# Gated linear attention into a multiplicative FFN on one core: K transposed by DMA instead of TensorE, state scaling on ScalarE, one block's products regrouped

## The chip, the cores and the metric

The kernel runs on one core of a Trainium2 chip. The metric is the device time of one execution in microseconds. Five engines work side by side, each through its own instructions in the order in which they were written: TensorE (PE; its weight loads are shown apart as PEld), VectorE (DVE), ScalarE (ACT), GpSimd (POOL), and SyncE (SP), which here issues every DMA. An instruction that waits holds up all that stands behind it on its engine.

## The reference

The first half is an attention with a gated state, the second a feed-forward block on its output. Sizes: batch 4, 8 heads, 768 tokens, head dimension 48; d_model 384, d_ff 1024; all in float32.

```python
f = 1.0 / (1.0 + np.exp(-f_logit))
for t in range(S):
    state = f[:, :, t, :, None] * state + np.einsum('bhd,bhe->bhde', k[:, :, t], v[:, :, t])
    y[:, :, t] = np.einsum('bhd,bhde->bhe', q[:, :, t], state)
x = y.transpose(0, 2, 1, 3).reshape(B * S, H * D)     # 3072 tokens by 384
a = x @ w1
b = x @ w2
h = a * b @ w3
out = h @ w_out
```

## The kernel before

**Attention.** The 3072 tokens are cut into 24 chunks of 128 (6 chunks make one batch element). A chunk's q, k and gate logits lie as 112 partitions (two heads of 48, the second from partition 64 on) by 512 columns (4 head pairs by 128 tokens). VectorE makes the running products of the gates forward and backward by two scans, and from them the scaled tiles Q and K (lines 545 and 559). The recurrence then becomes matmuls: K against Q gives the scores within a chunk (`pairs`), the masked scores A against v give the values inside the chunk (`values`), the state of the chunk before against Q gives the rest (`from_state`), and K against v gives the state's growth (`update`). The last of these sums over tokens, so it needs K with the tokens on partitions: a tile `kt`, 128 tokens by 4 x 112 columns. In the kernel before, TensorE turns K round with four transposes against an identity into a PSUM bank (`turn`, line 598), and ScalarE copies that bank to `kt` (line 731).

From chunk 4 on the matmuls of one chunk stand together with the next chunk's in one uninterrupted stretch on TensorE, called a visit here (`visit` in `rest`): values of chunk u, scores of chunk u+1, values again, the state's part, and the update of chunk u+1. So the visit of chunk u waits for Q, K and `kt` of chunk u+1. After it ScalarE copies the result (`outcome`, line 849) and the next scores (`taken`, line 707), GpSimd masks those (line 713), VectorE adds the state's growth (lines 763 and 766), and VectorE multiplies the state by the chunk's gate product G, one number per row and head pair (`state`, line 822). The result of a chunk goes through DRAM to be laid out anew as x for the FFN (lines 870 and 873).

**FFN.** The tokens form 6 blocks of 512. w3 and w_out are folded into one matrix early (line 1471). The up products (x by w1 and w2) of a block are then done in one of three ways: block 0 plainly (line 902), later ones by schemes with fewer products. `seven` (line 998) takes two column tiles of the hidden layer and makes their products with 22 matmuls of 128 by 256; a block has four such groups. `many` (line 1153) takes four column tiles with 40 such matmuls; a block has two such groups. `many` needs sums of weight columns (line 1114), which are kept in tiles that the attention used before, so it can start only once the attention is nearly through; the list `homes` names these tiles. In the kernel before, blocks 1 and 2 use `seven`, blocks 3 to 5 use `many`, and block 2 (counted from 0; `MANY - 1`, the third block) is mixed: two groups of `seven` and one of `many`. The down products (`down`, line 902 with 128 by 192) of every block use seven products for two token tiles.

**Order.** A planner in the kernel (`Plan`) lists every task with an engine, an assumed cost, what it waits for, a priority and the buffers that it takes; it then places the tasks one after the other and emits them in that order. So a changed cost or task moves others on every engine. Up to a planned time of 130 us, gaps on TensorE are filled with matmuls on a constant tile (`idle`, line 402).

**Places that the change touches:** `turning` and `turn` (K's transpose), `front` (K's buffers and the task of line 559), `state` and `outcome` in `rest`, `moves` (a DMA as a task on SP and one on the DMA engines), the `mixed` case of `ffn`, and the pools of `homes`.

Of the kernel before, what the change touches and what calls it, by code (L numbers as in the profile page):

```python
# [79 lines left out]
SURE_W = 2.0  # L80
NEED = (0.0, 1.0, 2.0, 3.0)
# [214 lines left out]
def ranged(ctx, tc, q, k, f_logit, v, w1, w2, w3, w_out, out, ident, w12, wc, left):  # L296
# [63 lines left out]
    homes += [lambda p=p, nm=nm: p.tile([P, NQ], F32, name=nm) for p, nm, n in ((one, "fwd", 1), (one, "bwd", 1), (work, "K", 2), (work3, "Q", 3), (work3, "ys", 3)) for _ in range(n)]  # L360
# [16 lines left out]
    plan.pools["t"][0:4] = [aside] * 4  # L377
# [89 lines left out]
    def moves(n, size, rate, emit, deps, prio, late=0.0, since=0.0, lanes=("lane",)):  # L467


        for j in range(n):  # L470
            i = plan.add("SP", 0.45, (lambda: None) if j else emit, [d] if j else deps, prio - j * 1e-3, takes=lanes, lag=0.85, since=since)
# [8 lines left out]
    def front(u):  # L480
# [76 lines left out]
        def scale_k():  # L557
            s["K"] = work.tile([P, NQ], F32, name="K")[0:R]
            nc.vector.tensor_tensor(s["K"], ku, s["R"], ALU.mult)  # L559

        t["k"] = plan.add("DVE", 0.72, scale_k, [t["r"], t["lk"]] + past(u, 2, "a", "t"), n0, shared=True)
# [162 lines left out]

    def turning(u):

        s, t = st[u], tk[u]

# [24 lines left out]
    def middle(u):  # L753
# [4 lines left out]
        def emit():  # L758
# [10 lines left out]
            "DVE", 0.36 if closes else 0.72, emit, [t["s"], t["m"]] + ([] if opens else past(u, 1, "d")) + past(u, 2, "v"), need(u) - 5,  # L769
        )  # L770

    def rest(u):
# [37 lines left out]
        if not closes:  # L810
# [8 lines left out]
            def state():  # L819
                gain = s["G"].unsqueeze(2).to_broadcast([R, HP, D])  # L820
                if u >= NPE:
                    nc.vector.tensor_tensor(s["S"], s["S"], gain, ALU.mult)
                    return
# [8 lines left out]
                "DVE", 0.36 if opens or u >= NPE else 0.72, state,  # L832
                [t["s"], t["G"]] + (past(u, 2, "b") if u < NPE else [t["mid"]]), n0, shared=True,
# [9 lines left out]
        def outcome():  # L843
            s["ys"] = work3.tile([P, NQ], F32, name="ys")[0:R].rearrange("p (h c) -> p h c", c=C)
            py = s["yb"] if u < NPE else s["py"][0:R, :, 0 : 2 * C]
            ys = s["ys"]
            if u >= NPE:
                ys, py = ys.rearrange("p (b r) c -> p r b c", r=2), py.rearrange("p r (b c) -> p r b c", c=C)
            nc.scalar.activation(ys, py, AF.Copy, accum_out=ysum[:, u : u + 1])  # L849
# [3 lines left out]
            "ACT", 0.8, outcome, [t["v"]] + past(u, 3, "z"),  # L853
# [35 lines left out]
        else:  # L889
            t["z"] = moves(2, 197, 300, written, [t["y"]], n0 - 100)  # L890
# [16 lines left out]
    def ffn(n):  # L907
# [655 lines left out]
    def judge():  # L1563
        low = work.tile([R, 1], F32, name="low")
        nc.vector.tensor_reduce(out=low, in_=lasts, axis=AX.XY, op=ALU.min)
        zero = work.tile([R, NU], F32, name="zero")
        nc.vector.tensor_scalar(zero, ysum, 0.0, None, ALU.mult)
        nil = work.tile([R, 1], F32, name="nil")
        nc.vector.tensor_reduce(out=nil, in_=zero, axis=AX.X, op=ALU.add)
        nc.vector.tensor_scalar(nil, nil, 0.0, None, ALU.is_equal)  # L1570
        good = work.tile([P, 1], F32, name="good")
# [11 lines left out]
    def heard():  # L1583
        row = work.tile([1, P], F32, name="row")
# [3 lines left out]
    def decided():  # L1588
        least = work.tile([1, 1], F32, name="least")
# [4 lines left out]
    for u in range(NU):  # L1594
# [13 lines left out]
        if u == NU - 1:  # L1608
            late = plan.add("none", 0.0, lambda: None)
            plan.pools["f"] += [late] * 4  # L1610
            for nm in ("y", "mid", "m", "v"):
                tk[u][nm]["frees"].append(late)
            fronts["deps"] += [tk[u][nm] for nm in ("r", "k", "q")] + [tk[u - 1]["G"]]
# [405 lines left out]
```

## Time and profile before

| | |
|---|---|
| median of 3 runs | 458.17 us (457.83 to 459.44) |
| the profiled execution's own time | 458.04 us |
| its span, first to last instruction | 456.2 us |
| PE busy | 448.7 us, 98% of the span |
| DVE / ACT / POOL busy | 371.1 / 212.0 / 69.1 us |
| granted TensorE clock | 1.00 in every stretch |
| visits that need a `kt` of chunk 7 or later | from 116.2 us to 246.9 us |
| last visit (chunk 23) starts | 251.5 us |

The profiled execution's time is its span and 1.84 us around it. Three stages are to be told apart: up to about 116 us the weights come in, are converted and folded, and the first chunks run; from there to 251.5 us the other chunks run with FFN work of blocks 0 to 2 between their visits; after that only FFN work is left, with checks on the weights' range in ScalarE's gaps. A busy share says little by itself: the question is always which engine the others wait for in a stage.

### The profile page before, as it was taken

To read this page: it belongs to the slowest core of one execution; us is meant where nothing else is said; L and a number is where in the kernel's file an instruction comes from. 1 tells how busy PE (TensorE), PEld (TensorE's weight loads), DVE (VectorE), ACT (ScalarE), POOL (GpSimd) and SP (SyncE) were. 2 spreads that over 40 slices of the span, in tenths; PEclk is the share of its full clock that TensorE was granted. 3 is DMA by queue.
4 is the path that set the end of the run, shared out by engine and by line. 5 is a ranking of instruction groups with operands and counts; after the bars stand their busy time and mean duration, and the time that the engine had idled before them with its cause. 6 is when DMAs were issued, how large, how long until landed. Compare 5 with 4: busy or idle time off the path is not lost.

```text
span 456.2 us, 11781 instructions
## 1 busy us (share of the span) xinstructions
PE 448.7 (98%) x4792; PEld 392.5 (86%) x4792; DVE 371.1 (81%) x651; ACT 212.0 (46%) x473; POOL 69.1 (15%) x90
## 2 busy tenths in 40 slices
PE   7999999999999999999999999999999999999996
PEld 6788886666899888889999888899899988889996
DVE  8997899999898999989999699885659466767641
ACT  4565344432234453443323256665665666675300
POOL 9341000131222531223223000000000000000000
PEclk9999999999999999999999999999999999999999
DMA  6897898833236666356323502446365612233111
GB/s 178 268 339 249 300 340 284 271 108 105 71 100 196 180 175 162 105 155 184 97 73 82 147 16 78 138 141 205 132 194 172 204 60 96 91 93 92 37 69 39
DMA packets 43308, 68.74 MB, mean 151 GB/s; under 512 B 5217, under 2 KB 28386, under 8 KB 42226
## 3 DMA queue, kind: packets, MB, share of 16 engines
q1 hardware_dynamic: 43250, 67.95, 48.6%
q8 instruction: 38, 0.62, 0.6%
q14 instruction: 20, 0.16, 0.1%
HBM read 58.88 MB, written 9.04 MB: 149 GB/s over the span
## 4 chain that ended last, share of the span: by engine, by line
PE 95%; DVE 1%; SPq 1%; DMA 1%; POOL 0%; issue 0%; POOLq 0%; DVEq 0%
PE f L902 25%; PE l L1153 15%; PE f L998 13%; PE f L1153 12%; PE f L1471 9%; PE l L902 9%; PE py L658 3%; PE pa L584 2%; PE f L598 2%; PE py L677 2%; PE pa L690 2%; PE f L402 1%; SPq L495 1%; DMA ab<-in_k_dram 1%; DVE K L559 0%
## 5 line engine op out<-in xcount | busy, mean ns | idle before, releaser
L713 POOL TENSOR_SCALAR_AFFINE_SELECT A<-A 64x512 f32<-64x512 f32 (+1 forms) x46 | 46.2, 1004 | 107.8 <-ACT A L707 105.7
L1471 PE MATMUL f<-place 128*128 128x384 f32 x128 | 42.4, 487 | 0.0
L902 PE MATMUL f<-xt,w 128*128 128x256 f32 x192 | 42.1, 380 | 0.0
L902 PEld LDWEIGHTS f<-xt,w 128*128 128x128 f32 x192 | 36.3, 190 | 5.0
L1471 PEld LDWEIGHTS f<-place 128*128 128x128 f32 x128 | 23.9, 190 | 15.5
L902 PE MATMUL f<-place 128*128 128x192 f32 x176 | 31.9, 327 | 0.0
L998 PE MATMUL f<-xt,w 128*128 128x256 f32 x120 | 31.3, 380 | 0.0
L551 DVE TENSOR_TENSOR_SCAN bwd<-gate,back 112x512 f32<-112x512 f32 x24 | 30.4, 1267 | 0.7
L529 DVE TENSOR_TENSOR_SCAN fwd<-gate,floor 112x512 f32<-112x512 f32 x24 | 30.0, 1251 | 1.2 <-ACT gate L521 0.3
L902 PEld LDWEIGHTS f<-place 128*128 128x128 f32 x176 | 28.9, 190 | 0.4 <-issue 0.2
L849 ACT ACTIVATE ys<-py 112x512 f32<-112x512 f32 x22 | 13.1, 597 | 32.4 <-PE py L677 29.9
L1407 ACT ACTIVATE place<-place 128x512 f32<-128x512 uint32 (+2 forms) x24 | 21.4, 890 | 9.7 <-DMA place<-in_w_dram 8.7
L998 PEld LDWEIGHTS f<-xt,w 128*128 128x128 f32 x120 | 22.5, 190 | 2.9
L902 PE MATMUL f<-wc,ab 128*128 128x192 f32 x128 | 23.6, 328 | 0.0
L813 POOL TENSOR_TENSOR G<-lasts,gate 112x4 f32<-112x4 f32 x20 | 12.3, 614 | 72.3 <-ACT lasts L534 28.7
L902 PEld LDWEIGHTS f<-wc,ab 128*128 128x128 f32 x128 | 21.2, 190 | 0.3
L521 ACT ACTIVATE gate<-f 112x512 f32<-112x512 f32 x22 | 13.9, 631 | 16.4 <-DVE bwd L551 7.2
L902 PE MATMUL l<-place 128*128 128x192 f32 x112 | 19.8, 326 | 0.0
L658 PEld LDWEIGHTS py<-A,vt 64*64 64x64 f32 (+1 forms) x672 | 13.3, 127 | 7.3 <-issue 6.3
L998 PE MATMUL f<-place 128*128 128x256 f32 x72 | 19.1, 386 | 0.0
L902 PEld LDWEIGHTS l<-place 128*128 128x128 f32 x112 | 18.5, 190 | 0.1
L658 PE MATMUL py<-A,vt 64*64 64x64 f32 (+1 forms) x672 | 18.0, 223 | 0.2
(288 smaller groups left out, 1063.4 us busy)
## 6 DMA issues: line engine op xcount, KB each, us to landing
place<-in_w_dram SPq DMA_DIRECT2D x21, 512.0 KB, 5.9
A<-in_w_dram SPq DMA_DIRECT2D x19, 512.0 KB, 4.0
place<-in_w_dram SPq DMA_DIRECT2D x8, 1024.0 KB, 6.3
q<-in_q_dram SPq DMA_DIRECT2D x46, 96.0 KB, 2.9
vt<-in_v_dram SPq DMA_DIRECT2D x23, 192.0 KB, 2.9
out_dram<-o SPq DMA_DIRECT2D x23, 192.0 KB, 2.8
k<-in_k_dram SPq DMA_DIRECT2D x44, 96.0 KB, 2.4
yt<-ys SPq DMA_DIRECT2D x44, 96.0 KB, 2.9
```

Source lines behind the costliest of these rows:

```text
L521: nc.scalar.activation(gate[u % 2][:, 0:NQ], fu, AF.Sigmoid)
L529: nc.vector.tensor_tensor_scan(s["P"], gate[u % 2][:, 0:NQ], floor, 0.0, ALU.mult, ALU.max)
L551: nc.vector.tensor_tensor_scan(s["R"][:, ::-1], gate[u % 2][:, NQ:0:-1], back[:, ::-1], 0.0, ALU.mult, ALU.max)
L658: done = nc.tensor.matmul(y_block(u, hp, par, half)[p0 : p0 + w], lhsT=s["v"][half * W : half * W + W, h * D : h * D + w], rhs=s["A"][half ...
L713: nc.gpsimd.affine_select(out=a, in_=a, pattern=pattern, compare_op=ALU.is_ge, fill=0.0, base=0, channel_multiplier=-1,)
L813: nc.gpsimd.tensor_tensor(s["G"], lasts[:, u], heads(gate[(u + 1) % 2][:, 0:NQ])[:, :, 0], ALU.mult)
L849: nc.scalar.activation(ys, py, AF.Copy, accum_out=ysum[:, u : u + 1])
L902: nc.tensor.matmul(out_, lhsT=lhs[i], rhs=rhs[i], start=start and i == 0, stop=i == len(lhs) - 1, skip_group_check=True,)
L998: nc.tensor.matmul(q[nm][:, which * TH : which * TH + TH], lhsT=lhs[i](which), rhs=rhs[i], start=start and which == 0 and i == 0, stop=i = ...
L1153: nc.tensor.matmul(banks[g, c][:, which * TH : which * TH + TH], lhsT=lhs, rhs=x_node(a), start=first and which == 0, stop=True, skip_grou ...
L1407: nc.scalar.activation(part_.bitcast(F32), part_, AF.Copy, bias=2.0, scale=2.0**-51)
L1471: nc.tensor.matmul(w3s["p", jc], lhsT=w3s[jc][:, kc * P : kc * P + P], rhs=wos[:, kc], start=(kc == 0), stop=(kc == KF - 1),)
```

## The change

From chunk 7 on (17 chunks, 7 to 23) `turning` calls a new function, `crossing`. ScalarE splits K's float32 words into 16-bit halves, first all of one half, then all of the other (`split`, into a part of tile A that is no longer used otherwise); one DMA transpose on SP's queue turns the 112 by 1024 halves into 128 by 8 x 112 (`crossed`); ScalarE puts the halves together again as `kt` (`merged`). There is one tile for the split halves and one for the transposed ones, so a split waits for the transpose before it, and a transpose for the merge before it. K gets three buffers instead of two, the results `ys` two instead of three.

The scaling of the state by G goes, from chunk 2 on, from one VectorE instruction to four ScalarE activations, one for each head pair with its own scale column (18 chunks). The third block's up products are now all by `seven`: four groups, none of `many`. The rest is what goes with it: tiles moved to make room, `homes` in a new order that the temporaries of `many` take only when the last chunks are done, and a planned margin (0.8) on the transfer of the results to DRAM.

```diff
-    diag = [t[:, 0 : 2 * HP * W].rearrange("p (r h c) -> p r h c", r=2, h=HP) for t in flat]
-    mids = [t[0:R, 2 * HP * W : 2 * HP * W + HP * D].rearrange("p (h d) -> p h d", d=D) for t in flat]
+    apart = both[0:R, 2 * (NQ + HP * D) : 2 * (NQ + HP * D) + NQ].bitcast(U16)
+    halves = keep.tile([P, HP * R], F32, name="halves").bitcast(U16)
+    diag = [both[:, i * NQ : i * NQ + NQ].rearrange("p (r h c) -> p r h c", r=2, h=HP) for i in range(2)]
+    mids = [both[0:R, 2 * NQ + i * HP * D : 2 * NQ + (i + 1) * HP * D].rearrange("p (h d) -> p h d", d=D) for i in range(2)]
...
-    plan.pools["t"][0:4] = [aside] * 4
+    held = plan.add("none", 0.0, lambda: None)
+    plan.pools["t"] = [aside] * 4 + [held] * (len(homes) - NWT)
...
-            s["K"] = work.tile([P, NQ], F32, name="K")[0:R]
+            s["K"] = work3.tile([P, NQ], F32, name="K")[0:R]
...
-        t["k"] = plan.add("DVE", 0.72, scale_k, [t["r"], t["lk"]] + past(u, 2, "a", "t"), n0, shared=True)
+        t["k"] = plan.add("DVE", 0.72, scale_k, [t["r"], t["lk"]] + past(u, 3, "a", "t"), n0, shared=True)
...
+    def crossing(u):
+        s, t = st[u], tk[u]
+        def split():
+            nc.scalar.copy(apart.rearrange("p (two n) -> p two n", two=2), s["K"].bitcast(U16).rearrange("p (n two) -> p two n", two=2))
+        def crossed():
+            nc.sync.dma_start_transpose(halves.rearrange("p (g r) -> p g r", r=R), apart)
+        def merged():
+            s["kt"] = work.tile([P, HP, R], F32, name="kt")
+            to = s["kt"].rearrange("p h r -> p (h r)").bitcast(U16).rearrange("p (n two) -> p two n", two=2)
+            nc.scalar.copy(to, halves.rearrange("p (two n) -> p two n", two=2))
+        n0 = need(u)
+        t["t"] = plan.add("ACT", 1.05, split, [t["k"]] + past(u, 1, "c2"), n0 - 50)
+        t["c2"] = moves(1, 74, 200, crossed, [t["t"]] + past(u, 1, "e"), n0 - 100, SURE_K, issue=1.23)
+        t["e"] = plan.add("ACT", 1.21, merged, [t["c2"]] + past(u, 2, "s"), n0 - 50)
...
+        if u > 6:
+            crossing(u)
+            return
...
-                    nc.vector.tensor_tensor(s["S"], s["S"], gain, ALU.mult)
+                    for hp in range(HP):
+                        nc.scalar.activation(s["S"][:, hp], s["S"][:, hp], AF.Copy, scale=s["G"][:, hp : hp + 1])
...
-                "DVE", 0.36 if opens or u >= NPE else 0.72, state,
+                *(("DVE", 0.36 if opens else 0.72) if u < NPE else ("ACT", 0.95)), state,
...
-            s["ys"] = work3.tile([P, NQ], F32, name="ys")[0:R].rearrange("p (h c) -> p h c", c=C)
+            s["ys"] = work.tile([P, NQ], F32, name="ys")[0:R].rearrange("p (h c) -> p h c", c=C)
...
-            t["z"] = moves(2, 197, 300, written, [t["y"]], n0 - 100)
+            t["z"] = moves(2, 197, 300, written, [t["y"]], n0 - 100, SURE_Z)
...
-            for jc in range(KH // 2 if mixed else KH):
+            for jc in range(KH):
                 seven(jc)
             if mixed:
-                many(1)
```

What this does to the order is shown at three places. In the rows, names with a number are single buffers of a tile; the line numbers of the changed kernel are some 5 to 31 higher than those before.

First TensorE, the end of one visit in the middle of the attention stage and what comes behind it. py is the PSUM tile of the results, pa that of the scores and the state's growth, f a bank of the FFN. Before:

```order
L658 MATMUL py<-A,vt 48x64 x2
L677 MATMUL py<-Q,S 48x64 x8
L677 MATMUL py<-Q,A 48x64 x8
L690 MATMUL pa<-vt,kt 48x48 x16
L598 MATMUL f_1930<-ident,K 128x112 x4
L998 MATMUL f_1712<-xt,place 128x256 x4
L998 MATMUL f_1811<-place,w_59 128x256
```

And the end of a visit now:

```order
L663 MATMUL py<-A,vt 48x64 x2
L682 MATMUL py<-Q,S 48x64 x8
L682 MATMUL py<-Q,A 48x64 x8
L695 MATMUL pa<-vt,kt 48x48 x16
L1027 MATMUL f_2146<-place 128x256
L1027 MATMUL f_2146<-xt,w_59 128x256
```

The four transposes (line 598 before) are gone, and FFN products follow the visit at once.

Next ScalarE, the rows of about one and a half chunks while down products of a block run as well. ys is the result, the A that is written from pa the scores, and the A that is written from K the split halves. Before:

```order
L849 ACTIVATE ys,ysum<-py 112x2x2x128
L707 COPY A<-pa 128x512
L1276 COPY place<-f_2779 128x192
L521 ACTIVATE gate_95<-f_102 112x512
L1289 COPY o<-f_2779 128x192
L534 COPY lasts<-fwd 112x4
L731 COPY kt<-f_2830 128x448
L1039 COPY place<-f_2568 128x512
L521 ACTIVATE gate_96<-f_103 112x512
```

And now:

```order
L743 COPY kt<-halves 128x2x448
L1068 COPY a_106<-f_2501 128x512
L735 COPY A<-K 112x1024
L539 COPY lasts<-fwd 112x4
L1304 COPY place<-f_2524 128x192
L851 ACTIVATE S<-S,G 112x48 x4
L1317 COPY o<-f_2524 128x192
L526 ACTIVATE gate_96<-f_103 112x512
L743 COPY kt<-halves 128x2x448
L878 ACTIVATE ys,ysum<-py 112x2x2x128
L735 COPY A<-K 112x1024
L712 COPY A<-pa 128x512
```

A merge (`kt<-halves`), a split (`A<-K`) and the four state scalings stand in ScalarE's row for each chunk; the transposed tile of one chunk is merged just ahead of the split for the next, and here both stand ahead of the copy of the scores.

Last SP's queue, the same stage in the changed kernel; the DMA to yt writes a chunk's result to DRAM, the one to xt reads it back:

```order
L738 DMA_TRANSPOSE halves<-A 128x8x112
L483 DMA vt<-in_v_dram 128x384
L500 DMA f_103<-in_f_logit_dram 48x512 x2
L899 DMA yt<-ys 48x4x128 x2
L500 DMA k_100<-in_k_dram 48x512 x2
L500 DMA q_97<-in_q_dram 48x512 x2
L500 DMA f_102<-in_f_logit_dram 48x512 x2
L902 DMA xt<-yt 128x3x128
```

One transpose for each chunk now stands among the loads and the result's two transfers; the rest of the queue has the same transfers as before, in a slightly other order.

More of the change, by code (lines that the diff above doesn't have):

```diff
@@ L80 @@
 SURE_W = 2.0
+SURE_K = 1.0
+SURE_Z = 0.8
 NEED = (0.0, 1.0, 2.0, 3.0)
@@ L1583, in heard @@
     def heard():
-        row = work.tile([1, P], F32, name="row")
+        row = one.tile([1, P], F32, name="row")
         nc.sync.dma_start(row, where["all"].rearrange("r one -> one r"))
@@ L1588, in decided @@
     def decided():
-        least = work.tile([1, 1], F32, name="least")
+        least = one.tile([1, 1], F32, name="least")
         nc.vector.tensor_reduce(out=least, in_=where["row"], axis=AX.X, op=ALU.min)
```

23 lines of the change are left out of this document (13 added, 10 removed).

## The prediction

> **What bounds the kernel now.** I read the page's busy times, slices and chain first. The chain is the work that ended last, followed back from the end.
>
> ```profile
> span 456.2 us, 11781 instructions
> ...
> PE 448.7 (98%) x4792; PEld 392.5 (86%) x4792; DVE 371.1 (81%) x651; ACT 212.0 (46%) x473; POOL 69.1 (15%) x90
> ...
> PEclk9999999999999999999999999999999999999999
> ...
> PE 95%; DVE 1%; SPq 1%; DMA 1%; POOL 0%; issue 0%; POOLq 0%; DVEq 0%
> ```
>
> TensorE is 95% of the chain at full granted clock. Then the two stages that the change touches, as busy time in a stretch (columns: length, then PE, PEld, DVE, ACT, POOL busy), and all that TensorE waited for:
>
> ```profile
> 116.20:251.50 135.30, 135.30 (x2637) 122.50 (x2636) 125.68 (x222) 53.17 (x130) 39.64 (x47) 1.00 0.49 134
> 251.50:456.20 204.70, 200.39 (x1097) 184.79 (x1096) 139.51 (x291) 108.19 (x247) 0.00 (x0) 1.00 0.35 111
> ...
> PE f L402 <- DVE floor L425: 1.7, 1, 1.7
> PE py L598 <- DVE K L559: 0.5, 1, 0.5
> PE f L598 <- DVE K L559: 0.5, 1, 0.5
> ```
>
> The first stage holds the visits from chunk 6 on; TensorE is busy in all 135.30 us of it, and all its waits in the whole kernel come to 2.7 us, none in this stage. In the second it is idle 4.3 us, at the very end, when the last outputs are stored. VectorE is close behind in the first stage (125.68 of 135.30 us), ScalarE far (53.17). So the kernel is TensorE's instruction list, and time goes only where that list gets shorter, or where it starts to wait.
>
> **The change, part by part.** *Removed: 17 groups of four transposes.* The pieces of the chain in order of time (start, length, what):
>
> ```profile
> 154.54 0.35 PE pa L690 x16
> 154.89 1.92 PE f L998 x8
> 156.81 0.38 PE f L598 x4
> 157.20 2.61 PE f L998 x12
> ...
> 161.33 0.36 PE pa L690 x32
> 161.69 0.53 PE f L598 x4
> 162.22 4.33 PE f L998 x20
> ...
> 219.67 1.74 PE f L998 x8
> ```
>
> A group costs 0.38 us amid FFN work and 0.53 us right behind a visit (whose last piece is pa L690). But eight FFN records take 1.92 us behind a visit and 1.74 us elsewhere: 0.18 us is the price of leaving a visit, and the FFN work will pay it once the transposes are gone. So a group behind a visit saves 0.35 us. In the timeline 10 of the 17 stand amid FFN work and 7 behind a visit: 10 x 0.38 + 7 x 0.35 = 6.25 us. Bounds: 17 x 0.35 = 5.95 us if all are of the cheaper kind, 17 x 0.53 = 9.0 us if the handover vanishes too.
>
> *Changed: the third block.* Two groups of `seven` (44 matmuls) replace one of `many` (40). Twenty records take 4.33 us, and a matmul has two records: 0.433 us each, so 4 x 0.433 = +1.73 us.
>
> *One saving that is given back.* Ahead of block 0's down products the planner fills a gap with matmuls on a constant, in the old order and in the new, so something other than TensorE sets the time there:
>
> ```profile
> 117.91 5.38 PE f L902 x24
> 123.29 0.86 PE f L402 x4
> ```
>
> The first of the 17 groups stands before this point, so its 0.35 us only lengthens that gap.
>
> The sum goes against the profiled execution's own 458.04 us (span 456.2 and 1.84 around it; the runs' median is 458.17): 458.04 - 6.25 + 1.73 + 0.35 = 453.9 us.
>
> *Added on ScalarE.* The trace has no copy of 16-bit halves; the nearest rows (busy us, mean ns of one):
>
> ```profile
> L731 ACT COPY kt<-f 128x448 f32<-128x448 f32 x22 | 11.8, 537 | 7.0 <-PE f L598 6.8
> L704 ACT COPY A<-pa 128x1024 f32<-128x1024 f32 x2 | 2.0, 1008 | 0.0
> L1407 ACT ACTIVATE place<-place 128x1024 f32<-128x1024 uint32 x8 | 9.3, 1165 | 7.3 <-DMA place<-in_w_dram 7.3
> L534 ACT COPY lasts<-fwd 112x4 f32<-112x4 f32 x24 | 4.8, 202 | 8.1 <-DVE fwd L529 8.1
> L1289 ACT COPY o<-f 128x192 f32<-128x192 f32 x8 | 2.5, 319 | 13.6 <-PE f L902 13.6
> L1039 ACT COPY a<-f 128x512 f32<-128x512 f32 x9 | 5.3, 585 | 5.1 <-PE f L998 4.9
> L1042 ACT COPY ab<-f 128x256 f32<-128x256 f32 x6 | 2.2, 372 | 7.5 <-PE f L998 7.5
> L713 POOL TENSOR_SCALAR_AFFINE_SELECT A<-A 64x512 f32<-64x512 f32 (+1 forms) x46 | 46.2, 1004 | 107.8 <-ACT A L707 105.7
> L822 DVE TENSOR_TENSOR S<-S,G 112x192 f32<-112x192 f32 x18 | 7.3, 404 | 0.6
> ```
>
> The split has 1024 elements a row: 1.01 us plain, 1.17 us with strided words; I take the middle, 1.09, since it reads with a stride and writes dense. The merge has 896: 0.95 us at the same rate. A state scaling of 48 columns lies between 0.20 us (4 columns) and 0.32 us (192): 0.23, four of them 0.92. The old copy of `kt` (0.54) goes. Per chunk +2.42 us, 17 times 41 us. The new order also draws 36 more matmuls of `seven` between these visits (22 go with three copies of 0.585 and one of 0.372): +3.5 us. The stage itself becomes 135.3 - 5.9 + 36 x 0.433 = 145 us. So ScalarE has 98 us of work in 145: busier than before, not full. This costs nothing as long as TensorE's other work in the list covers a copy that comes later; without that cover each chunk could lose a few tenths (a rival below).
>
> *Taken from VectorE:* 18 x 0.40 = 7.3 us. TensorE never waited for it there, so that gains nothing by itself. The scaled state comes 0.92 - 0.40 = 0.5 us later; the visit that reads it also waits for the mask, whose two GpSimd instructions take 2 x 1.0 us over the same time, and these hide it.
>
> *Added on SP and the DMA queue.* 17 transposes of 112 x 2048 bytes, 224 KB. The trace has none; its DMAs, from issue to landing:
>
> ```profile
> vt<-in_v_dram SPq DMA_DIRECT2D x23, 192.0 KB, 2.9
> xt<-yt SPq DMA_DIRECT2D x22, 192.0 KB, 3.4
> ...
> place<-in_w_dram SPq DMA_DIRECT2D x21, 512.0 KB, 5.9
> place<-in_w_dram SPq DMA_DIRECT2D x8, 1024.0 KB, 6.3
> ...
> place<-in_v_dram SPq DMA_DIRECT2D x1, 192.0 KB, 8.9
> ...
> good<-good SPq DMA_DIRECT2D x1, 0.5 KB, 7.9
> ```
>
> Below, 2.9 us (192 KB in long rows); above, 7.9 us (128 pieces of 4 bytes, the smallest pieces in the trace). Nearest is xt<-yt, short pieces and almost the size: 3.4 x 224 / 192 = 4.0 us.
>
> What it must fit into is a ring: split (one tile for the halves), transpose, merge (one tile for the result), next split. I put it at 1.09 + 4.0 + 0.95 and 0.5 us of hops = 6.5 us per chunk. The visits must be at least that far apart. A visit takes 2.08 us (0.38 + 0.47 + 0.23 + 0.45 + 0.36, and the 0.18 behind it):
>
> ```profile
> 159.80 0.38 PE py L658 x11
> 160.18 0.47 PE pa L584 x30
> 160.65 0.23 PE py L658 x16
> 160.88 0.45 PE py L677 x32
> ...
> 298.48 0.86 PE l L1153 x4
> 299.34 1.30 PE l L902 x8
> ```
>
> Between the start of chunk 9's visit and that of chunk 22's, the new order has 13 visits, 140 matmuls of `seven`, 2 of `many` (four records 0.86, so 0.43 us each) and 56 down matmuls (eight records 1.30, so 0.325 us each): 27.0 + 60.6 + 0.9 + 18.2 = 106.7 us, 8.2 us per chunk; the shortest distance is 2.08 + 10 x 0.433 = 6.4 us. A ring of 6.5 us fits, with 0.1 us short once or twice, which the second `kt` buffer evens out. So I cost the transposes at nothing; TensorE's FFN work hides them, by a margin of 1.7 us per chunk.
>
> [...]
>
> **Rivals.** *1. The ring becomes the bound (slower).* If a transpose takes longer to land, visits wait for `kt`, and with them all that stands behind in TensorE's list. For it: one tile each for halves and result, SP's one queue in which a transpose can stand behind a result's store that waits, and the 512 KB loads at 5.9 us. Against: 8.2 us between visits. At 5.9 us the ring is 8.4: the six distances from chunk 9 on average 7.7 us (78 `seven` matmuls, six visits), the last five 7.9 us, so 6 x 0.7 + 5 x 0.5 = 6.7 us are lost: 460.6 us. That is the point from which it is slower; at 6.3 us it loses 11 us: 465. I price it at 463 us.
>
> *2. ScalarE's row holds TensorE up a little (no change).* A merge and a split, 2.04 us, stand ahead of the copies of scores and FFN banks, and a late transpose holds up everything behind its merge. A `seven` group has 4 matmuls (1.73 us) between the one that ScalarE copies and the one that needs the copy (0.585): 2.04 + 0.585 - 1.73 = 0.9 us short where the pair falls right there. At once in three chunks, 17 x 0.3 = 5 us: 458.9 us. For it: 68% busy in written order. Against: the order interleaves two groups.
>
> [...] With 7.9 us, the price of the 4-byte pieces, the ring is 10.4 us: 13 x (10.4 - 8.2) = 29 us, 483 us. Against: that DMA moves 0.5 KB; all others land within 6.3 us in the median but for one load of 8.9 us in the crowded first 20 us. [...]
>
> That the change doesn't do what it says is out: in the new order the 17 groups are gone.
>
> **Numbers.** The forecast, 453.9 us, gets 0.60, with its own range from 450.7 (9.0 us saved, nothing given back) to 455.8 us. Rival 2 gets 0.18, rival 1 0.17, rival 3 0.05. What a measurement here can tell from no change is about 0.5%, 2.3 us. So faster 0.60, same 0.18, slower 0.22. The range is 450.5 to 461: it takes in rival 2 and the near half of rival 1.
>
> **What would show it.** Right: no L598 after chunk 6; TensorE without idle time between 116 us and the last visit, which starts some 9 us later than 251.5; a transpose landing near 4 us; splits and merges near 1 us; ScalarE near 98 us in the stage. Wrong: waits of py L663 or pa L695 for ACT kt L743, or visits spaced evenly at the ring's length (rival 1); waits of f L1027 for ACT copies (rival 2); landings of 8 us and more (rival 3). If the span between two visits shrinks by more than 0.38 us for a group, my price of a transpose is wrong.

## The result, and the profile after

The changed kernel takes 456.76 us (median of 11 runs, 455.17 to 458.17); the kernel before, timed in turn with it, 459.25 us (457.83 to 459.55). The ratio is 0.995, with a 95% interval of 0.9933 to 0.9966. So the change gains some 2.5 us; the interval leaves 1.6 to 3.1 us. The prediction said 453.9 us, 0.9% less than before. On two further occasions the changed kernel gave 0.9933 (0.9912 to 0.9955) and 0.996 (0.9937 to 0.9984) of before.

The first view is the page: span, busy times, DMA totals, the main DMA queue (packets, MB, share of 16 engines' span) and the chain that ended last. Of the changed kernel:

```profile
span 456.0 us, 11696 instructions
PE 445.6 (98%) x4732; PEld 388.5 (85%) x4732; DVE 357.5 (78%) x615; ACT 249.1 (55%) x557; POOL 67.2 (15%) x90
DMA packets 59086, 72.65 MB, mean 159 GB/s; under 512 B 20994, under 2 KB 44163, under 8 KB 58003
q1 hardware_dynamic: 59026, 71.85, 56.6%
PE 88%; DVE 4%; POOL 3%; DMA 1%; ACT 1%; issue 1%; SPq 1%; DVEq 0%; POOLq 0%
```

And the two DMA lines of the kernel before:

```profile
DMA packets 43308, 68.74 MB, mean 151 GB/s; under 512 B 5217, under 2 KB 28386, under 8 KB 42226
q1 hardware_dynamic: 43250, 67.95, 48.6%
```

TensorE was 95% of the chain and is now 88%; VectorE, GpSimd, ScalarE and DMA have 9% together. TensorE still stands out, but the end now also hangs on other engines. The 17 transposes bring 15,778 packets, nearly all under 512 bytes.

Next, both stages (length, then PE, PEld, DVE, ACT, POOL busy, granted clock, DMA share, GB/s) and waits inside the first one (engine, tile and line, what it waited for: us, times, longest):

```profile
118.30:265.70 147.40, 145.95 (x2646) 130.51 (x2645) 129.21 (x224) 92.09 (x206) 36.49 (x47) 1.00 0.67 146
265.70:456.00 190.30, 185.79 (x1029) 172.09 (x1028) 123.13 (x257) 100.34 (x236) 0.00 (x0) 1.00 0.37 121
...
ACT kt L743 <- DMA halves<-A: 16.4, 9, 3.4
DVE place L1001 <- DMA xt<-yt: 2.4, 1, 2.4
PE pa L589 <- DVE S L794: 0.8, 1, 0.8
PE pa L695 <- ACT kt L743: 0.5, 1, 0.5
```

The attention stage was forecast at 145 us and takes 147.4. TensorE, which waited for nothing there before, now waits for VectorE's state sum (L794) and once for `kt`; the first places to look are the two long waits above, ScalarE's for transposes (halves) and VectorE's for one gather (xt).

All stages side by side, each row from one profiled execution, with the visits' starts read from the timeline (us; chunk 3's matmuls come alone, before the joint visits):

| kernel | chunk 3 starts | to chunk 6 | to the last visit | to the end | from chunk 3 on |
|---|---|---|---|---|---|
| before | 34.1 | 82.1 | 135.3 | 204.7 | 422.1 |
| changed | 35.2 | 83.1 | 147.4 | 190.3 | 420.8 |
| changed, second occasion | 34.3 | 83.1 | 146.4 | 189.9 | 419.4 |
| changed, third occasion | 34.8 | 83.6 | 147.0 | 190.2 | 420.8 |
| transposes cut to an eighth | 34.4 | 83.4 | 144.9 | 190.0 | 418.2 |
| changed, sums later | 34.5 | 83.5 | 146.0 | 190.0 | 419.4 |
| changed, rows exchanged on SP | 34.5 | 83.6 | 146.7 | 190.0 | 420.3 |
| changed, both of these | 33.9 | 84.1 | 145.1 | 190.1 | 419.4 |
| both, again | 34.4 | 83.2 | 145.4 | 190.3 | 419.0 |

The start of chunk 3 varies by a microsecond between executions of one kernel, so the last column compares best. The forecast, 4.17 us less, would be 417.9 there. The tail fell by 14.4 to 14.8 us, since FFN work went from it into the attention stage: 68 records, or 34 matmuls, fewer in the last row of the view above than in the prediction's. The stretch to chunk 6 is one to two microseconds longer in all of them. One of these is no loss but moved work: behind chunk 3 TensorE now makes 156 records of the first block's products in one go instead of 150, and has the six fewer to make in the attention stage. Before, and in the changed kernel:

```profile
35.47 32.64 PE L902 MATMUL f<-xt,w 128*128 128x256 f32 x150
...
36.59 33.94 PE L931 MATMUL f<-xt,w 128*128 128x256 f32 x156
```

What is missing in the changed kernel lies for the most part in the third column: 1.4 to 2.4 us above the forecast 145. In its first profile TensorE counts as idle for 1.45 us of the 2.4 (147.40 less 145.95). The experiments look for the missing time.

### The profile page after: what moved, and what is told of

Its sections match the earlier page's. It is cut to its first block, busy times and chain, and to the rows that moved or that the text cites. A ratio compares the mean times of both kernels' runs of the same rounds, so it can differ in the third digit from the quotient of the medians.

```text
span 456.0 us, 11696 instructions
## 1 busy us (share of the span) xinstructions
PE 445.6 (98%) x4732; PEld 388.5 (85%) x4732; DVE 357.5 (78%) x615; ACT 249.1 (55%) x557; POOL 67.2 (15%) x90
## 3 DMA queue, kind: packets, MB, share of 16 engines
q1 hardware_dynamic: 59026, 71.85, 56.6%
## 4 chain that ended last, share of the span: by engine, by line
PE 88%; DVE 4%; POOL 3%; DMA 1%; ACT 1%; issue 1%; SPq 1%; DVEq 0%; POOLq 0%
PE f L931 25%; PE f L1027 13%; PE f L1182 11%; PE l L1182 11%; PE f L1499 9%; PE l L931 8%; PE py L663 3%; PE pa L589 2%; PE py L682 2%; PE pa L695 1%; POOL ab L445 1%; DMA xt<-yt 1%; DVE fwd L534 1%; POOL A L718 1%; DVE K L564 1%
## 5 line engine op out<-in xcount | busy, mean ns | idle before, releaser
L931 PE MATMUL f<-xt,w 128*128 128x256 f32 x192 | 42.1, 380 | 0.0
L1027 PE MATMUL f<-xt,w 128*128 128x256 f32 x160 | 40.8, 380 | 0.0
L931 PEld LDWEIGHTS f<-xt,w 128*128 128x128 f32 x192 | 36.4, 190 | 4.9
L1499 PEld LDWEIGHTS f<-place 128*128 128x128 f32 x128 | 23.9, 190 | 15.3
L931 PE MATMUL f<-place 128*128 128x192 f32 x200 | 36.6, 329 | 0.1
L1027 PEld LDWEIGHTS f<-xt,w 128*128 128x128 f32 x160 | 30.4, 190 | 4.0
L931 PEld LDWEIGHTS f<-place 128*128 128x128 f32 x200 | 32.9, 190 | 0.9 <-PE f L931 0.3
L534 DVE TENSOR_TENSOR_SCAN fwd<-gate,floor 112x512 f32<-112x512 f32 x24 | 30.5, 1273 | 2.7 <-ACT lasts L539 1.1
L743 ACT COPY kt<-halves 128x896 uint16<-128x896 uint16 x17 | 20.4, 1199 | 16.4 <-DMA halves<-A 16.4
L1027 PE MATMUL f<-place 128*128 128x256 f32 x96 | 25.5, 388 | 0.0
L851 ACT ACTIVATE S<-S,G 112x48 f32<-112x48 f32 x72 | 18.2, 327 | 10.9 <-DVE S L794 10.3
L663 PEld LDWEIGHTS py<-A,vt 64*48 64x48 f32 (+1 forms) x672 | 13.6, 127 | 8.3 <-issue 6.3
L550 DVE TENSOR_TENSOR Q<-q,fwd 112x512 f32<-112x512 f32 x23 | 16.0, 694 | 4.8 <-PE py L682 4.8
L1027 PEld LDWEIGHTS f<-place 128*128 128x128 f32 x96 | 17.5, 190 | 2.4 <-ACT a L1068 0.2
L663 PE MATMUL py<-A,vt 64*48 64x64 f32 (+1 forms) x672 | 18.4, 223 | 0.7 <-POOL A L718 0.5
```

The lines of the kernel that those rows point to most:

```text
L534: nc.vector.tensor_tensor_scan(s["P"], gate[u % 2][:, 0:NQ], floor, 0.0, ALU.mult, ALU.max)
L550: nc.vector.tensor_tensor(s["Q"], qu, s["P"], ALU.mult)
L663: done = nc.tensor.matmul(y_block(u, hp, par, half)[p0 : p0 + w], lhsT=s["v"][half * W : half * W + W, h * D : h * D + w], rhs=s["A"][half ...
L743: nc.scalar.copy(to, halves.rearrange("p (two n) -> p two n", two=2))
L851: nc.scalar.activation(s["S"][:, hp], s["S"][:, hp], AF.Copy, scale=s["G"][:, hp : hp + 1])
L931: nc.tensor.matmul(out_, lhsT=lhs[i], rhs=rhs[i], start=start and i == 0, stop=i == len(lhs) - 1, skip_group_check=True,)
```

## The experiments

**The changed kernel again** (no edit), beside the three that follow.

> The changed kernel once more, as the base of this group. All theories: 0.995 of before within 0.002; in the trace the same three losses (about 1 us before 36 us, waits of PE of about 1.3 us between 160 and 210 us, DMA share near 1 from 180 to 220 us) if they belong to the kernel and not to one execution.

It took 455.95 us, 0.9933 of before (459.0). Its place in the table shows that the missing time isn't a constant: 1.4 us in the stage, not 2.4.

**What a transpose on TensorE costs.** The kernel before, with each group of four from chunk 7 on issued twice:

```diff
-        for hp in range(HP):
+        for hp in [*range(HP)] * (2 if u > 6 else 1):
             nc.tensor.transpose(
```

> The kernel before with the four transposes of chunks 7 to 23 done twice into the same bank; nothing else changes, nor the order. My price: a group amid FFN work costs 0.38 us, so 17 x 0.38 = 6.5 us more than before (ratio 1.014). Rival, that a group costs TensorE much less than the chain shows (half the gain was never there): about 3 us more (ratio 1.007).

It took 465.15 us, 1.0135 (1.0117 to 1.0154). That is 6.2 us, or 0.365 us a group; the prediction's removal was 6.25 us. The price stands, so the gain is lost elsewhere.

**The transposes' traffic alone.** The kernel before, with 17 DMA transposes of K besides, into a part of A that nobody reads:

```diff
             nc.scalar.copy(s["kt"].rearrange("p (b two) r -> p b (two r)", two=2), s["pk"])
+            if u > 6:
+                nc.sync.dma_start_transpose(halves.rearrange("p (g r) -> p g r", r=R), s["K"].bitcast(U16))
```

> The kernel before, unchanged in its work, with the 17 DMA transposes of K issued as well, into a scratch tile that nobody reads, without the split, the merge and the planner's knowledge. If the transposes' load on the DMA queue costs the missing part of the gain: 1.5 to 3 us more than before (ratio 1.003 to 1.007), with DMA share near 1 where the chunks follow closest and later landings of xt. If the load is harmless and the ring or ScalarE's row costs it: within 0.5 us of before.

It took 459.34 us, 1.0016 (0.9994 to 1.0039): no difference that can be told. **Transposes cut to an eighth**: the changed kernel with one of the eight 112 by 128 blocks turned; the rest of the halves is set to zero once, so the state's growth from chunk 7 on isn't computed.

```diff
-            nc.sync.dma_start_transpose(halves.rearrange("p (g r) -> p g r", r=R), apart)
+            nc.sync.dma_start_transpose(halves[:, 0:R], apart[:, 0:P])
```

> The changed kernel with each DMA transpose cut to one of its eight blocks of 128 columns (the rest of the halves is zero, so the state's growth from chunk 7 on is not computed rightly); same order, same split and merge. If the transposes' load on the queue and their landing cost the missing part: 1.5 to 2.5 us less than the changed kernel (ratio to before 0.990 to 0.992), no wait of PE between 160 and 210 us. If what is missing lies on ScalarE or in the early stage: as the changed kernel (0.995).

It took 455.24 us, 0.9932 (0.9906 to 0.9957). In the medians that is 0.7 us less than the changed kernel beside it, within the noise; in the profile the stage takes 144.9 us, the forecast 145. The stretch from 160 to 220 us in four kernels (columns as above, DMA share last but one). Before:

```profile
160.00:220.00 60.00, 60.00 (x1207) 53.11 (x1196) 55.72 (x98) 26.43 (x65) 16.12 (x23) 1.00 0.57 156
```

The changed kernel:

```profile
160.00:220.00 60.00, 58.55 (x998) 51.55 (x988) 53.19 (x91) 40.48 (x92) 16.30 (x20) 1.00 0.94 183
```

With transposes cut to an eighth:

```profile
160.00:220.00 60.00, 60.00 (x1102) 53.63 (x1097) 54.17 (x92) 42.70 (x92) 17.68 (x19) 1.00 0.60 157
```

The kernel before with the traffic alone:

```profile
160.00:220.00 60.00, 60.00 (x1203) 52.77 (x1202) 55.88 (x98) 27.14 (x64) 16.73 (x23) 1.00 0.96 191
```

Full transposes fill the 16 DMA engines in this stretch (0.94 against 0.57), and only the changed kernel has TensorE idle there. But the same load costs the old order nothing that can be told (its stage takes 135.9 us instead of 135.3): what counts is what stands in the rows behind a late transfer. From chunk 6's visit on, the changed kernel and the cut one differ in four intervals between visits and agree within 0.02 us in the others (us from one visit's start to the next):

| interval that begins at about | 165 | 175 | 182 | 190 | 197 | 209 |
|---|---|---|---|---|---|---|
| cut to an eighth | 9.9 | 6.3 | 7.3 | 7.3 | 11.6 | 9.4 |
| changed | 10.6 | 6.3 | 8.4 | 7.6 | 11.9 | 9.4 |
| changed, second occasion | 10.3 | 6.3 | 7.7 | 7.6 | 11.9 | 9.4 |
| changed, third occasion | 10.1 | 6.3 | 8.5 | 7.6 | 11.9 | 9.4 |
| sums later | 9.9 | 6.3 | 8.3 | 7.3 | 11.6 | 9.4 |
| rows exchanged on SP | 9.9 | 6.3 | 8.4 | 7.6 | 11.9 | 9.4 |
| both | 10.1 | 6.3 | 7.3 | 7.3 | 11.6 | 9.4 |
| both, again | 10.4 | 6.3 | 7.3 | 7.3 | 11.6 | 9.4 |

The timeline of the changed kernel shows the largest, the one from 182.8 us, on four engines in turn: SP's queue, ScalarE, VectorE, TensorE (start, length, what; in brackets the idle time before it and what ended it).

```profile
174.76 0.86 SPq L899 DMA_DIRECT2D yt<-ys  x2
175.72 0.87 SPq L500 DMA_DIRECT2D q<-in_q_dram  x2
177.74 0.39 SPq L902 DMA_DIRECT2D xt<-yt  x1
178.22 2.63 SPq L738 DMA_TRANSPOSE halves<-A  x1
...
182.93 1.20 ACT L743 COPY kt<-halves 128x896 uint16<-128x896 uint16 x1 [3.00 <-DMA halves<-A]
...
178.96 0.68 DVE L550 TENSOR_TENSOR Q<-q,fwd 112x512 f32<-112x512 f32 x1
182.09 0.42 DVE L1001 TENSOR_TENSOR place<-xt 128x256 f32<-128x256 f32 x1 [2.44 <-DMA xt<-yt]
...
183.61 0.36 DVE L794 TENSOR_TENSOR S<-pa,A 112x192 f32<-112x192 f32 x1
...
184.02 0.69 PE L589 MATMUL pa<-Q,K 48*64 48x64 f32 x32 [0.80 <-DVE S L794]
```

The result of chunk 11 goes out at 174.76; SP waits until it has landed, and only then, at 177.74, starts the gather that reads it back. The next K transpose stands behind that gather in SP's queue. Both land late. VectorE makes four sums of that xt (for the third block's `seven`), and three of them stand in its row ahead of the state sum; it waits 2.44 us, the state sum frees the bank that the next scores need, and TensorE waits. ScalarE meanwhile waits 3.00 us for the transpose, with a split and the FFN's copies behind the merge.

The same place with transposes cut to an eighth (SP, then VectorE; the same rows in the same order):

```profile
171.77 0.86 SPq L901 DMA_DIRECT2D yt<-ys  x2
...
174.63 0.39 SPq L904 DMA_DIRECT2D xt<-yt  x1
175.12 1.09 SPq L740 DMA_TRANSPOSE halves<-A  x1
...
177.82 0.42 DVE L1003 TENSOR_TENSOR place<-xt 128x256 f32<-128x256 f32 x1
...
180.12 0.36 DVE L796 TENSOR_TENSOR S<-pa,A 112x192 f32<-112x192 f32 x1
```

VectorE doesn't wait for xt there. From the store to the gather SP takes 2.9 us, and 3.0 us in the changed kernel; but the store goes out 3.6 us ahead of the next visit (at 175.3 us), and in the changed kernel 1.8 us ahead (visit at 176.5 us). So SP's row is already late when it reaches this store. The issue of a transpose, 1.09 us for an eighth and 1.22 to 1.28 us for most full ones, explains little of that; which of the transfers ahead of it delayed SP isn't shown.

**The four sums later.** In the changed kernel's plan these four rows of VectorE are held back. In its trace all four then stand behind the two state sums (L791, L794), a scan of the gates (L534) and a short gate row (L544); the scan has also come ahead of the state sums, where the expectation counts three rows and nothing else moved. The rows of every other engine are the same in the same order.

```diff
-                s["S", i] = plan.add("DVE", 0.43, emit, deps + last + w12_sums[-1:] + folds, 100 * n + 30)
+                s["S", i] = plan.add("DVE", 0.43, emit, deps + last + w12_sums[-1:] + folds, 100 * n + 30, slack=3.0 if n == 2 and i == 0 else 0.0)
```

> The changed kernel with one place altered: the four sums that VectorE makes of the third block's xt stand three rows (three state sums and a gate row) later in its order; every other row of every engine stands where it stood. Theory (the transposes' packets make the xt of chunk 11 land late, and VectorE, which takes its rows in order, holds the state sums and the gates behind that wait): no row of VectorE waiting 2 us or more for xt, a stage from chunk 6's visit to the last of about 145 us instead of 146.4 to 147.4, and 454.5 to 455.3 us, against 455.95 of the changed kernel on that chip (0.990 to 0.992 of before). Rival (the missing time is spread over the intervals, by the ring of split, transpose and merge or by chance): 0.993 to 0.995 of before and a stage still above 146.

It took 456.98 us, 0.9956 (0.9939 to 0.9972): nothing gained, and my theory as it stood fell: VectorE's wait for xt shrank to 1.1 us, but the stage takes 146.0 us. The intervals at 190 and 197 us came back, and the large one stayed at 8.3 us. (The one at 165 us came back too, but it ends before the moved rows, and varies from 9.9 to 10.6 us in the kernels that share its rows.) The timeline says why the large one stays (ScalarE, then TensorE):

```profile
182.03 1.24 ACT L743 COPY kt<-halves 128x896 uint16<-128x896 uint16 x1 [3.10 <-DMA halves<-A]
183.12 1.05 ACT L735 COPY A<-K 112x1024 uint16<-112x1024 uint16 x1
184.06 0.59 ACT L1068 COPY place<-f 128x512 f32<-128x512 f32 x1
...
184.71 1.99 PE L1027 MATMUL f<-xt,place 128*128 128x256 f32 x8 [0.81 <-ACT place L1068]
```

With VectorE out of the way, TensorE waits 0.81 us for ScalarE's copy of an FFN bank, which stands behind the late merge and the split: the prediction's second rival, at one place. So there is a second late row, and either alone costs the interval.

**The transpose ahead of the gather.** Two neighbouring rows of SP exchanged and nothing else, alone and together with the later sums:

```diff
+    listing = plan.order()
+    late_xt = tk[11]["x"]["deps"][0]
...
+    listing.remove(late_xt)
+    listing.insert(listing.index(moved_past) + 1, late_xt)
-    for t in plan.order():
+    for t in listing:
```

> The changed kernel with two neighbouring rows of SyncE's order exchanged, and nothing else: the gather of xt of chunk 11, which waits there for yt to land, now stands behind the K transpose that stood behind it. Theory (a transpose that stands in SyncE's row behind a gather that waits makes the merge late, and ScalarE's row holds a feed-forward copy behind the merge): ScalarE's wait of 3 us for halves shrinks to under 1 us, the interval between visits that took 8.4, 7.6 and 8.3 us in the three profiles takes 7.2 to 7.4 us, and the time falls by 0.4 to 1.2 us against the changed kernel on this chip. The xt of chunk 11 lands a little later, so VectorE's wait for it stays (2 us or more) and with it the 0.5 us of the interval that begins at about 165 us. Rival (the transposes land late because the DMA queues are full, wherever they stand): the wait and the interval stay.

> The changed kernel with the exchange on SyncE and, besides, VectorE's four sums of the third block's xt three rows later, as in the run that did that alone. Theory: both losses gone, all intervals between visits within 0.2 us of those of the kernel with transposes cut to an eighth, 418.3 to 418.8 us from chunk 3's visit to the end, 454.4 to 455.2 us, 0.990 to 0.991 of before. Rival (what one place gives back, the next takes, as when the sums alone were moved): 419.4 us or more, 0.993 to 0.996 of before.

> The changed kernel unaltered, on the chip of the two others: 0.993 to 0.996 of before. By the theory its profile loses time against the kernel with the cut transposes in the intervals that begin at about 165, 182, 190 and 197 us and nowhere else by more than 0.2 us; by the rival that the losses are spread by chance, in others.

Measured beside each other (before 458.72 us): the exchange alone 457.74 us, 0.9981 (0.9963 to 0.9999); both 455.18 us, 0.9932 (0.9908 to 0.9957); the changed kernel 457.19 us, 0.996 (0.9937 to 0.9984), with its losses in the four intervals and no others. Alone the exchange gains nothing, against what I expected of it: ScalarE's wait halves, but VectorE waits as long for xt as before (2.60 us), and its row decides as it did. With both, the intervals at 182, 190 and 197 us are those of the cut kernel, and the stage takes 145.1 us. But from chunk 3 on it takes 419.4 us, which was the rival's figure and not the 418.3 to 418.8 us of the theory: the stretch to chunk 6, which the edit doesn't touch, took 84.1 us in this profile. The rows of the exchange alone:

```profile
180.60 1.21 ACT L743 COPY kt<-halves 128x896 uint16<-128x896 uint16 x1 [1.51 <-DMA halves<-A]
...
181.25 0.43 DVE L1001 TENSOR_TENSOR place<-xt 128x256 f32<-128x256 f32 x1 [2.60 <-DMA xt<-yt]
...
183.19 0.69 PE L589 MATMUL pa<-Q,K 48*64 48x64 f32 x32 [0.82 <-DVE S L794]
```

**Both once more:**

> The kernel with both rows moved, once more, on another occasion. Theory: 0.991 to 0.994 of before again, where the changed kernel gave 0.995, 0.993 and 0.996, and in its profile the intervals that begin at about 182, 189 and 197 us are again 7.2 to 7.4, 7.2 to 7.3 and 11.6 us. Rival (the first run of it was a lucky one): 0.994 to 0.996, and at least one of these intervals 0.3 us or more longer.

455.87 us, 0.9932 (0.9908 to 0.9956), and the intervals as expected. Its rows at the same place (SP, ScalarE, VectorE, TensorE):

```profile
175.74 1.22 SPq L738 DMA_TRANSPOSE halves<-A  x1
177.07 0.52 SPq L902 DMA_DIRECT2D xt<-yt  x1
...
179.22 1.21 ACT L743 COPY kt<-halves 128x896 uint16<-128x896 uint16 x1
...
180.38 0.36 DVE L794 TENSOR_TENSOR S<-pa,A 112x192 f32<-112x192 f32 x1
...
181.59 0.42 DVE L1001 TENSOR_TENSOR place<-xt 128x256 f32<-128x256 f32 x1 [0.76 <-DMA xt<-yt]
...
182.22 0.64 PE L589 MATMUL pa<-Q,K 48*64 48x64 f32 x32
```

Counted from the visit before, the merge starts 2.9 us earlier than in the changed kernel, the state sum comes before the wait, and TensorE doesn't stop. The DMA load is the same; only two rows stand elsewhere. By the profiles this gives 1.6 us from chunk 6's visit to the end (335.5 us on average, 337.1 in the three profiles of the changed kernel). In the medians it is 2.0 us where both ran side by side; the changed kernel's best occasion, 0.9933, is as good. It is the fastest version found, by a margin that doesn't fully part it from the changed kernel in the intervals; against the kernel before both occasions agree.

**The three parts of the change apart.** K on TensorE again (`u > 99` in place of `u > 6`), the other two parts as in the change:

> The changed kernel with K transposed by TensorE in every chunk, as before; the state is still scaled by ScalarE and the third block's up products are still all by sevens. By the prediction's terms: four matmuls more, 1.73 us, and nothing for the state's step, so about 460.8 us (1.004 of before). Rival (VectorE's rows hold up the visits, and a lighter VectorE lets them through): 458 to 459 us, 0.998 to 1.000. Second rival (the third block's way matters by more than its four matmuls, since its sevens need VectorE's sums of xt): 462 us or more.

459.78 us, 1.0016 (1.0006 to 1.0027). The other two parts together cost 0.7 us instead of the 1.73 us of my sum; so the way of K is worth some 3 us of the possible 5.9, with the order planned anew for each. **The third block mixed again**, the rest as in the change:

```diff
-            for jc in range(KH):
+            for jc in range(KH // 2 if mixed else KH):
                 seven(jc)
             if mixed:
+                many(1)
```

> The changed kernel with the third block's up products mixed again, as before (two columns by sevens, two in the other way); transposes and state as in the change. By the prediction's terms: four matmuls fewer, so 1.73 us less than the changed kernel: about 454.2 us (0.9895 of before), if the matmuls between the visits are enough of a fill without the extra sevens. Rival (the stage lacks matmuls that can go, or the order written for it sets a long row ahead of a visit): no gain, 0.993 to 0.998.

467.47 us, 1.0196 (1.0163 to 1.0229): far slower than either expectation. The stretches of its timeline around the end of the stage, and a wait there:

```profile
240.00:252.00 12.00, 12.00 (x295) 10.38 (x293) 10.96 (x21) 8.13 (x19) 1.59 (x3) 1.00 0.37 58
252.00:258.00 6.00, 3.17 (x29) 2.44 (x28) 5.76 (x13) 2.11 (x5) 1.47 (x2) 0.98 0.14 36
258.00:264.00 6.00, 3.52 (x98) 3.17 (x98) 5.83 (x14) 2.23 (x7) 1.49 (x2) 0.50 0.14 36
264.00:270.00 6.00, 5.21 (x69) 4.28 (x70) 5.86 (x12) 0.69 (x2) 0.16 (x1) 0.50 0.46 126
...
PE pa L589 <- DVE S L794: 3.5, 1, 3.5
```

The last three visits start at 250.1, 254.7 and 263.2 us, with 12 records of `many` (2.8 us) between the first two and no other work for TensorE between the last two. Within the second of them TensorE waits 3.5 us for a state sum, and during this wait its granted clock falls to 0.50, until about 271 us (from 270 to 280 us it is 0.93 on average). VectorE isn't idle: from 251.2 to 257.8 us it makes sums for `many` (L1149 and others), which stand ahead of this state sum in its row. So both halves of the rival are seen: the stage lacks matmuls that can go, and a long row stands ahead of a visit. In this order the third block's sevens aren't a cost of 1.73 us; they are work that the stage needs. Whether another order would do without them isn't shown.

**The state on VectorE again**, one operation (and its task in the plan with it), the rest as in the change; in effect:

```diff
-                    for hp in range(HP):
-                        nc.scalar.activation(s["S"][:, hp], s["S"][:, hp], AF.Copy, scale=s["G"][:, hp : hp + 1])
+                    nc.vector.tensor_tensor(s["S"], s["S"], gain, ALU.mult)
```

> The changed kernel with the state scaled by VectorE in one operation, as before, in all chunks. The prediction costs the step at nothing: 0.992 to 0.995 of before, the same as the changed kernel within 0.3 us or so. Rival (TensorE's waits in the stage go back to VectorE's order, and about 11 us more on it lengthen them): a stage of 148 us or more and 457 us or more (0.996 and up). Second rival (ScalarE's row is what the merges and the copies of the feed-forward's results stand behind): faster, 0.989 to 0.991.

457.92 us, 0.9985 (0.9959 to 1.0011), where the changed kernel gave 0.9933 to 0.996 on three occasions: 1.1 to 2.4 us slower by these ratios, though the intervals touch. Its stage takes 154.1 us and its tail 185.7 us, so more FFN work stands ahead of the last visit. Its TensorE waits in the stage are other ones, and the granted clock (last but two in the third row) is 0.52 in one stretch:

```profile
PE pa L696 <- ACT kt L744: 1.1, 1, 1.1
PE f L1031 <- ACT a L1072: 0.8, 1, 0.8
152.00:155.50 3.50, 3.50 (x9) 2.79 (x10) 3.36 (x4) 2.17 (x5) 0.29 (x1) 0.52 0.70 173
```

The first rival's signs came (a stage over 148 us, a time over 457 us), but not its cause: both waits are for ScalarE, none for VectorE. The slow clock costs about 1.7 us in this execution (0.48 of 3.5 us, an estimate from the third row). It isn't in all of them: eight of the twelve have a mean clock of 0.998 or more, and their median is 457.5 us. The order was planned anew, so this prices the step together with its order, not VectorE's 7 us alone.

## Why the prediction was right or wrong

- **What bounds the kernel, and the price of a removed group:** right. Twice the groups cost 6.2 us, the sum had 6.25.
- **Prices on ScalarE:** near, and without effect by themselves. They are the same in the kernel with cut transposes, which loses nothing in the stage. By the rows below a merge takes 1.20 us (0.95 forecast), a split 1.04 (1.09), four scalings 1.01 us in the timeline (0.92); ScalarE has 92 us of work in the stage (98).
- **The landing and the ring:** right. A transpose lands in 3.8 us in the median (3.1 to 4.7), where 4.0 was worked out from xt's 3.4. The visits aren't spaced by the ring and TensorE waits for `kt` once, 0.5 us, so rival 1 is out; with no landing near the 7.9 us of rival 3, that one too. With transposes cut to an eighth the median landing is 3.1 us, 0.7 us less than with all eight blocks. Beside the gathers of the same profile (xt 4.1 us) the landing is no longer, while the time that the DMA engines are held is (last section). No run shows the ring's 0.5 us of hops as such: from the end of a split to the issue of its transpose the changed kernel has between 0.02 and 4.06 us.

```profile
L743 ACT COPY kt<-halves 128x896 uint16<-128x896 uint16 x17 | 20.4, 1199 | 16.4 <-DMA halves<-A 16.4
L735 ACT COPY A<-K 112x1024 uint16<-112x1024 uint16 x17 | 17.7, 1041 | 0.4 <-DVE place L1310 0.4
...
xt<-yt SPq DMA_DIRECT2D x22, 192.0 KB, 4.1
halves<-A SPq DMA_TRANSPOSE x17, 3.8
```

- **The step that failed:** "So I cost the transposes at nothing; TensorE's FFN work hides them, by a margin of 1.7 us per chunk." The margin is an average over a ring of three steps. What it left out is that the steps stand in rows with other work: the transpose behind a gather that waits on SP, the FFN's copies behind the merge on ScalarE, and, with SP's row and the gather late, the sums of xt ahead of the state sum on VectorE. In the prediction's sum this term was nothing; it measured 1.4 to 2.4 us in the stage (146.4 to 147.4 us against 145). Cutting the transposes takes all of it away (144.9 us), and moving two rows takes away most (145.1 and 145.4 us). That full transposes cause the loss and these rows decide it is shown by this; how full ones make SP's row late, by the load on the DMA engines or otherwise, stays open. Rival 2 named ScalarE's row, but priced it over all chunks; it decided at one place, and only together with VectorE's.
- **"So that gains nothing by itself"**, of VectorE's relief: neither borne out nor refuted. Without it the kernel is 1.1 to 2.4 us slower, but with a new order, and with waits for ScalarE and a slow clock in its profile, not waits for VectorE. What is shown is that VectorE's row can hold TensorE once the margin is thin: in the changed kernel TensorE waits 0.80 us for its state sum (L794 above), and before it waited for nothing there.
- **The third block's +1.73 us:** the price of a matmul was right (34 fewer in the tail, 14.4 to 14.8 us), the step wasn't a step of its own. Without it the kernel loses some 11 us (1.0196 against 0.995 of before), part of it by the granted clock of 0.50 from about 257.7 to 271 us.
- **The stage's length:** 145 us forecast, 144.9 with cut transposes. That the last visit starts 14.2 us later, not some 9, is 9.7 us of this, the 2.4 us of the failed step, and 2.1 us that had come before chunk 6. The 145 us came out although six records fewer and six others more (four of `many`, two of `idle`) stand in the stage than the sum had; these happen to even out.
- **The base:** the sum started from a profiled execution of 458.04 us; in the comparisons the kernel before has medians of 458.7 to 459.25 us. This is about a microsecond of the distance between 453.9 and 456.76 us, and the failed step is of the size of the rest.

Still open is a part of a microsecond. With both rows moved the medians are 3.5 and 3.0 us better than before, the sum said 4.17. In its profiles 0.2 and 0.5 us remain in the interval at 165 us, in which TensorE waits 0.5 us for `kt` in the changed kernel and 0.3 us in the second of these profiles: the wait that rival 1 named, at one place. The rest can't be placed: single executions of most kernels with K by DMA spread over 3 us and more (455.17 to 458.17 for the change), those of the kernel with K on TensorE and the other two parts over 1.2 us (459.61 to 460.77), and of each run one execution was profiled.

## What to carry to other kernels

Costing a new transfer by its landing time and the distance between its users isn't enough: list what stands behind each of its steps in every engine's row, SP's queue included, and ask what happens when it lands a microsecond or two late. When an edit frees the bound engine, ask again how far it is ahead of the next engines: here TensorE waited for nothing in the stage before and for 0.80 and 0.5 us after, and without the fill of matmuls the changed kernel took 467.47 us. Ask too whether two late rows meet at one place: here, with either moved alone, the interval stayed at 8.3 or 8.4 us, and with both it took 7.3 us.

## What the runs showed of the hardware

- The 17 transposes of 224 KB raise the main queue's share from 48.6% of 456.2 us to 56.6% of 456.0 us: 221.7 to 258.1 us of all 16 engines, so 2.1 us each, with what they add to other transfers' packets (1.7 us in the profile with both rows moved, 2.1 in the one with the traffic alone). The kernel before moves 67.95 MB in 221.7 us, by which 224 KB would take 0.75 us, an estimate. Each transpose is 928 packets (15,778 by 17), nearly all under 512 bytes. The landing, 3.8 us beside the gathers' 4.1, shows nothing of this.
- In the second profile with both rows moved, the transpose at 175.74 us held SP's queue for 1.22 us and the gather behind it for 0.52 us. In the kernel with transposes cut to an eighth, the two at 175.12 and 181.33 us held it for 1.09 us each, so the size mattered little here. Over the 17 of the changed kernel it was 1.22 to 2.63 us, 1.28 in the median; no run shows why the one at 178.22 us took 2.63 us.
- In the kernel with the third block mixed, the granted clock fell to 0.50 at about 257.7 us, some 2.5 us into TensorE's wait of 3.5 us, and stayed there for about 13.7 us; these are estimates from the clock of the stretches, 0.98 from 252 to 258 us, 0.50 from 258 to 270 and 0.93 from 270 to 280 us. With the state on VectorE it was 0.52 from 152.0 to 155.5 us, in a stage with two waits of TensorE of 1.1 and 0.8 us. The changed kernel's wait of 0.80 us left it at 1.00 (182.8 to 184.0 us), and the profile with the later sums has 1.00 on average with a wait of 0.81 us. What sets the length of the slow stretches isn't shown.
